# One directly loaded chunk in place of two, its transfers divided by partitions over two queues

## The chip, the cores and the metric

The kernel runs on one core of one Trainium2 chip. The metric is the device time of one execution in microseconds (us); lower is better. The four executions shown took between 714.0 and 714.33 us, with a median of 714.04 us.

The core has these engines: TensorE for matmuls (PE in the profile, its weight loads apart as PEld), VectorE (DVE), ScalarE (ACT), GpSimd (POOL) and SyncE (SP). DMA transfers are issued by an engine onto its queue and carried out by 16 DMA engines. In this kernel SyncE and ScalarE issue onto a hardware queue each (q1 and q10 in the profile), GpSimd onto a software queue (q0). The loads on GpSimd's queue can change the type on the way, here from fp32 to fp16.

## The reference

Two stages, one feeding the other. The first is a cross-covariance attention over channels, for each of 4 batches; the second an MLP with a squared ReLU over all 24320 tokens.

```python
# q, k, v: (4, 6080, 256) float32, tau = 1.0
qn = q / (np.linalg.norm(q, axis=1, keepdims=True) + 1e-06)
kn = k / (np.linalg.norm(k, axis=1, keepdims=True) + 1e-06)
s = kn.transpose(0, 2, 1) @ qn / tau            # 256 x 256 for each batch
a = softmax(s, axis=-1)
x = (v @ a).reshape(24320, 256)
h = x @ w_in                                    # 256 -> 2048
r = np.maximum(h, 0.0)
out = (moe_s * (r * r) + moe_b) @ w_out         # 2048 -> 256
```

## The kernel before, in words

For each batch the kernel needs the 256 x 256 product of k and q over 6080 rows (the Gram matrix) and the sums of squares of every column of q and k. From these it makes the attention matrix and folds it into w_in at once, so that the MLP's first matmul takes v directly: `wa` is that folded weight, and `mm1` (line 751) multiplies it with v transposed. The MLP runs in 48 groups of 512 tokens (the last of 256) and 16 steps to a group; the batches after the first have their Gram work laid between these steps by a table of step numbers (`at_step`). Batch 0 can't be hidden that way: nothing of the MLP can start before its Gram matrix is complete. It is worked through ahead of the loop, and this is the part that the change touches.

Batch 0's rows are cut into 13 chunks: 11 of 512 rows (128 partitions, 4 rows each), one of 256 and one of 192 (96 partitions). A chunk has two transfers, k and q. `Gram.load` (lines 120 to 134) issues them in one of two ways:

- Chunks below `NDIRECT` (line 97) are loaded directly: k by SyncE's queue and q by ScalarE's, as fp32, 512 KB each, into the staging tile `raw32` (line 491), which lies in a slot of the pool that later holds the MLP's activations. `Gram.cast` then makes fp16 of them: DVE casts k (line 139), ACT casts q (line 140).
- All others are loaded by GpSimd's queue (line 133), which casts on the way: 512 KB of fp32 are read and 256 KB of fp16 written.

GpSimd issues in program order: chunks 2 to 9, k and q of each in turn; then k of the last three chunks and q of the last three; then v's first group, five pieces of w_in, and v, w_out and two scalars. The chunks' fp16 tiles come from a pool of 8 buffers (`qk_pool`), which w_out's four pieces use afterwards.

For each chunk but the last three, the order of work on the engines (lines 551 to 559) is: eight matmuls of the Gram matrix (line 149, two for each of 4 rows); on some chunks one or two matmuls on constant data (`keep_busy`, line 544); squares of k on ACT (line 180); squares of q on DVE for even chunks (line 177) and on ACT for odd ones; two folding additions on DVE (line 194), and one that adds the result to chunk 0's (line 208). The last three chunks, the late ones, are ordered so that k's norms are complete first: squares, matmuls that sum them over the partitions (line 247), and four small ACT operations that make the inverse norm (line 272), while q of these chunks is still being loaded. Then come q's norms (line 251), the scaling, the exponentials and the first block of `wa` (lines 297 to 347), and with it the first MLP matmul.

Nearly every instruction is kept in program order on its engine (`po`). An engine that waits holds up all that stands behind it on that engine.

Of the kernel before, what the change touches and what calls it, by code (L numbers as in the profile page):

```python
# [17 lines left out]
def kernel(  # L18
# [12 lines left out]
    nc = tc.nc  # L31
    P = 128
# [23 lines left out]
    def po(ins):  # L56

        tc.keep_in_program_order(ins)
        return ins
# [34 lines left out]


    JC = 4
    NDIRECT = 2

    def make_chunks(rows_of):
        chunks, at = [], 0  # L100
# [11 lines left out]
    class Gram:  # L112
# [7 lines left out]
        def load(self, c, parts=(0, 1)):  # L120

            at, np_, jc = self.chunks[c]
            if 0 in parts:
                self.raw[c] = qk_pool.tile([P, 2, JC, C], FP16, tag="qk", name="qk")
            t = self.raw[c]
            direct = self.b == 0 and c < NDIRECT
            for i in parts:
                src = (k, q)[i]
                rows = src[self.b, at : at + np_ * jc, :].rearrange("(p j) c -> p j c", j=jc)
                if direct:  # L130
                    (nc.sync, nc.scalar)[i].dma_start(out=raw32[:, c, i], in_=rows)
                else:
                    po(nc.gpsimd.dma_start(out=t[:np_, i, :jc, :], in_=rows))
            self.tiles[c] = t[:, 1], t[:, 0]
# [355 lines left out]
    g0 = grams[0]  # L490
    raw32 = gpool.tile([P, NDIRECT, 2, JC, C], FP32, tag="g16", name="raw32")

# [4 lines left out]
    nc.vector.memset(eps, EPS)  # L497
    for c in range(NDIRECT):
        g0.load(c)
        g0.cast(c)  # L500
    for c in range(NDIRECT, len(g0.chunks) - NLATE):
        g0.load(c)
# [155 lines left out]
    for i, f in enumerate(folds):  # L658
        early.setdefault(FOLDS[i], []).append(f)
    at_step(14, lambda: po(nc.vector.tensor_scalar_mul(  # L660
        out=s_out, in0=s_bc, scalar1=1.0 / (LAM * LAM))))
# [357 lines left out]
```

## Time and profile before

| what | value |
|---|---|
| median of 4 executions | 714.04 us (714.0 to 714.33) |
| the profiled execution | 714.07 us, span 712.3 us from first to last instruction |
| TensorE's mean granted clock | 0.997 |
| PE busy | 693.0 us, 97% of the span |
| the two DVE casts of k, each | 0.69 us, starting at 5.98 and 9.59 us |
| the two ACT casts of q, each | 1.04 us, starting at 6.15 and 9.95 us |
| direct loads, issue to landing | 5.2 to 8.7 us |
| first and last issue of batch 0's loads on GpSimd | 1.42 and 26.43 us |
| first MLP matmul (L751) | 37.29 us |

Reading the profile: "L149" is line 149 of the kernel. A group's row gives the engine, the operation, the written tile, the read tile and the number of instructions. In square brackets or behind an arrow stands what ended the idle time before an instruction. A DMA share of 1 means that all 16 DMA engines had a packet in work throughout; it can pass 1, since packets of one engine overlap. GB/s counts the bytes written; a load that casts reads twice what it writes.

### The profile page before, as it was taken

To read this page: it belongs to the slowest core of one execution; us is meant where nothing else is said; L and a number is where in the kernel's file an instruction comes from. 1 tells how busy PE (TensorE), PEld (TensorE's weight loads), DVE (VectorE), ACT (ScalarE), POOL (GpSimd) and SP (SyncE) were. 2 spreads that over 40 slices of the span, in tenths; PEclk is the share of its full clock that TensorE was granted. 3 is DMA by queue.
4 is the path that set the end of the run, shared out by engine and by line. 5 is a ranking of instruction groups with operands and counts; after the bars stand their busy time and mean duration, and the time that the engine had idled before them with its cause. 6 is when DMAs were issued, how large, how long until landed. Compare 5 with 4: busy or idle time off the path is not lost.

```text
span 712.3 us, 17529 instructions
## 1 busy us (share of the span) xinstructions
PE 693.0 (97%) x7422; PEld 502.5 (71%) x7422; DVE 635.3 (89%) x905; ACT 548.5 (77%) x599; POOL 113.6 (16%) x192
## 2 busy tenths in 40 slices
PE   4699999999999999999999999999999999999998
PEld 2456777776677777777677777777768777777777
DVE  4889999999988989998999899998998888888886
ACT  5789877787787777778877777777876777777875
POOL 4533132202102222111010222111000000000000
PEclk9999999999999999999999999999999999999999
DMA  9999999556665977465761888637423333321202
GB/s 235 207 258 171 178 166 140 116 100 122 124 116 105 139 139 149 102 96 102 153 129 50 149 139 148 126 76 97 101 64 75 94 71 75 97 61 46 83 31 75
DMA packets 87838, 83.81 MB, mean 118 GB/s; under 512 B 56352, under 2 KB 62768, under 8 KB 87760
## 3 DMA queue, kind: packets, MB, share of 16 engines
q0 software_dynamic: 26992, 43.74, 38.1%
q1 hardware_dynamic: 60192, 37.71, 22.1%
q8 instruction: 58, 0.95, 0.6%
q10 hardware_dynamic: 576, 1.25, 0.5%
q14 instruction: 20, 0.16, 0.1%
HBM read 78.91 MB, written 24.90 MB: 146 GB/s over the span
## 4 chain that ended last, share of the span: by engine, by line
PE 95%; DMA 3%; ACT 1%; DVE 1%; issue 0%; DVEq 0%; ACTq 0%
PE h_ps L751 46%; PE o_ps L922 40%; PE s_ps L149 4%; DMA qk<-in_k_dram 1%; PE wa_ps L389 1%; DMA raw<-in_q_dram 1%; PE o_ps L826 1%; ACT sq L180 1%; PE o_ps L798 0%; PE wa_ps L331 0%; DVE f L194 0%; ACT r L272 0%; PE n_ps L247 0%; ACT qk L140 0%; DVE f L208 0%
## 5 line engine op out<-in xcount | busy, mean ns | idle before, releaser
L761 ACT ACTIVATE r<-h_ps 128x1024 f16<-128x1024 f32 (+1 forms) x384 | 388.5, 1013 | 144.2 <-PE h_ps L751 140.5
L751 PE MATMUL h_ps<-vT,wa 128*128 128x512 f16 (+7 forms) x1632 | 452.1, 364 | 0.5 <-ACT wa L324 0.5
L922 PEld LDWEIGHTS <-S 128*128 128x128 f16 x2944 | 198.1, 98 | 84.3
L922 PEld LDWEIGHTS <-g 128*128 128x128 f16 x2208 | 155.0, 98 | 74.1
L774 DVE TENSOR_TENSOR g<-r 128x2048 f16<-128x2048 f16 (+2 forms) x150 | 174.9, 1166 | 10.0 <-ACT r L761 9.5
L922 PE MATMUL o_ps<-T,S 128*128 128x128 f16 x2208 | 183.2, 219 | 0.0
L751 PEld LDWEIGHTS <-wa 128*128 128x128 f16 x1632 | 136.5, 98 | 19.0 <-ACT wa L324 1.0
L922 PE MATMUL o_ps<-w_out,g 128*128 128x128 f16 x1472 | 134.3, 219 | 0.0
L772 ACT ACTIVATE g<-r 128x1024 f16<-128x1024 f16 (+1 forms) x97 | 100.3, 1034 | 0.2
L779 DVE SCALAR_TENSOR_TENSOR o_sb<-o_ps,s_out,u 128x256 f32<-128x256 f32 x138 | 66.6, 482 | 36.0 <-PE o_ps L922 34.2
L149 PE MATMUL s_ps<-qk 128*128 128x256 f16 (+1 forms) x384 | 71.4, 287 | 14.5 <-ACT qk L140 9.2
L453 POOL DMA_DIRECT2D v<-in_v_dram x48 | 31.4, 663 | 238.7 <-DMA vT<-v 164.9
L210 POOL DMA_DIRECT2D f<-f x33 | 28.8, 874 | 248.1 <-DVE f L194 205.5
L779 DVE SCALAR_TENSOR_TENSOR u<-o_ps,s_out,rowconst 128x256 f32<-128x256 f32 x138 | 66.1, 479 | 0.0
L922 PE MATMUL o_ps<-w_out,S 128*128 128x128 f16 x736 | 63.5, 219 | 0.0
L922 PE MATMUL o_ps<-N,g 128*128 128x128 f16 x736 | 63.4, 219 | 0.0
L851 DVE TENSOR_TENSOR S<-S,g 128x2048 f16<-128x2048 f16 (+1 forms) x47 | 56.5, 1201 | 1.2
L180 ACT ACTIVATE sq<-qk 128x1024 f16<-128x1024 f16 (+2 forms) x53 | 54.5, 1041 | 3.9 <-DMA qk<-in_k_dram 2.2
L849 DVE TENSOR_TENSOR S<-g 128x2048 f16<-128x2048 f16 (+1 forms) x47 | 56.1, 1194 | 0.0
L855 DVE TENSOR_TENSOR S<-g,S 128x2048 f16<-128x2048 f16 x46 | 56.0, 1218 | 0.0
L853 DVE TENSOR_TENSOR S<-g 128x2048 f16<-128x2048 f16 x46 | 56.0, 1217 | 0.0
L149 PEld LDWEIGHTS <-qk 128*128 128x128 f16 (+1 forms) x384 | 32.7, 103 | 20.5 <-ACT qk L140 9.6
(103 smaller groups left out, 335.6 us busy)
## 6 DMA issues: line engine op xcount, KB each, us to landing
out_dram<-o_sb SPq DMA_DIRECT2D x43, 512.0 KB, 3.0
v<-in_v_dram POOLq DMA_DIRECT2D x47, 256.0 KB, 4.9
qk<-in_k_dram POOLq DMA_DIRECT2D x42, 256.0 KB, 6.6
qk<-in_q_dram POOLq DMA_DIRECT2D x42, 256.0 KB, 7.4
f<-f POOLq DMA_DIRECT2D x30, 128.0 KB, 2.9
vT<-v SPq DMA_TRANSPOSE x182, 3.1
w<-in_moe_w_out_dram POOLq DMA_DIRECT2D x4, 512.0 KB, 10.1
out_dram<-o_sb SPq DMA_DIRECT2D x8, 256.0 KB, 4.8
```

What stands on the lines that cost most here:

```text
L149: po(nc.tensor.matmul(self.s_ps[:, ch, :], qc[:np_, j, ts(ch, P)], kc[:np_, j, :], start=(c == 0 and j == 0 and ch == 0), stop=(c == len(s ...
L180: po(nc.scalar.activation(out=st["sq"][:np_, a, js, :], in_=(qc, kc)[a][:np_, js, :], func=AF.Square))
L751: po(nc.tensor.matmul(dst, wa[:, ci, ts(m, P)], src, start=(ci == 0), stop=(ci == CH - 1), skip_group_check=True))
L761: po(nc.scalar.activation(out=r16[:, :, i % 2, :n], in_=h_tiles.pop((g, i))[:, :, :n], func=AF.Relu))
L772: po(nc.scalar.activation(out=dst, in_=src, func=AF.Square))
L774: po(nc.vector.tensor_mul(dst, src, src))
L779: po(nc.vector.scalar_tensor_tensor(out=dst, in0=src, scalar=s_out, op0=ALU.mult, in1=add, op1=ALU.add))
L849: po(nc.vector.tensor_add(T[1], A21, A22))
L851: po(nc.vector.tensor_sub(T[2], T[1], A11))
L853: po(nc.vector.tensor_sub(T[3], A11, A21))
L855: po(nc.vector.tensor_sub(T[4], A12, T[2]))
L922: po(nc.tensor.matmul(st[name][:, j, :], a()[:, i, ts(j, P)], w[:, i, :], start=first, stop=last, skip_group_check=True))
```

## The change

`NDIRECT` goes from 2 to 1: only chunk 0 is loaded directly and cast by DVE and ACT, and chunk 1 goes by GpSimd's queue, ahead of chunk 2. `raw32` is half as large. Each of chunk 0's two transfers is divided by partitions: SyncE issues partitions 0 to 63 and ScalarE partitions 64 to 127, of k first and then of q. So SyncE and ScalarE still issue two transfers each, of 256 KB in place of 512 KB, and GpSimd issues two more than before. `ts(h, 64)` is the slice of 64 partitions from 64 h on; k is `i = 0`, q is `i = 1`.

```diff
     JC = 4
-    NDIRECT = 2
+    NDIRECT = 1
...
                 rows = src[self.b, at : at + np_ * jc, :].rearrange("(p j) c -> p j c", j=jc)
                 if direct:
-                    (nc.sync, nc.scalar)[i].dma_start(out=raw32[:, c, i], in_=rows)
+                    for h, queue in enumerate((nc.sync, nc.scalar)):
+                        ps = ts(h, P // 2)
+                        queue.dma_start(out=raw32[ps, c, i], in_=rows[ps])
                 else:
                     po(nc.gpsimd.dma_start(out=t[:np_, i, :jc, :], in_=rows))
```

## The prediction

> **What bounds the kernel now.** I read the page first, its busy shares and the shares of the chain that ended last, to see which stage the change touches; then the chain from its start; then the load stage in windows of 1 us, because a chain names one wait where several may stand behind each other. The page:
>
> ```profile
> PE 693.0 (97%) x7422; PEld 502.5 (71%) x7422; DVE 635.3 (89%) x905; ACT 548.5 (77%) x599; POOL 113.6 (16%) x192
> ...
> PE 95%; DMA 3%; ACT 1%; DVE 1%; issue 0%; DVEq 0%; ACTq 0%
> ```
>
> TensorE carries 95% of the chain, but not its beginning. The chain from the start, as start, length, what:
>
> ```profile
> 1.19 8.73 DMA raw<-in_q_dram
> ...
> 9.95 1.04 ACT qk L140
> ...
> 20.47 9.47 DMA qk<-in_k_dram
> 29.97 1.07 ACT sq L180
> ...
> 37.29 0.60 PE h_ps L751 x2
> ```
>
> Until the first MoE matmul at 37.29 us the chain hangs on batch 0's loads: the second direct load of q, then a GpSimd load of k issued at 20.47 and landed at 29.97. After 37.29 TensorE is busy without a break, so the change is worth the shift it gives to 37.29. Next, what the loads wait for (columns: window, length, busy time of PE, PEld, DVE, ACT, POOL, granted clock, DMA share, GB/s written):
>
> ```profile
> 2.00:3.00 1.00, 0.00 (x0) 0.00 (x0) 0.00 (x0) 0.02 (x1) 1.00 (x3) 1.00 0.72 111
> 3.00:4.00 1.00, 0.00 (x0) 0.00 (x0) 0.00 (x0) 0.00 (x0) 1.00 (x3) 1.00 0.95 356
> 4.00:5.00 1.00, 0.00 (x0) 0.00 (x0) 0.00 (x0) 0.00 (x0) 1.00 (x3) 1.00 1.04 426
> 7.00:8.00 1.00, 0.75 (x4) 0.57 (x5) 0.00 (x0) 0.19 (x1) 0.00 (x0) 1.00 1.07 352
> 20.00:21.00 1.00, 0.01 (x1) 0.00 (x0) 0.94 (x2) 0.69 (x2) 0.53 (x1) 1.00 1.11 207
> ```
>
> The DMA share is at 1 or above from 4 us on, and from 10 to 30 us the rate stays at 209 GB/s written. Those loads read fp32 and write fp16, so 209 written is 418 GB/s read; the direct loads write what they read, 426. Counted in fp32 bytes the 16 DMA engines do the same work either way, without a pause: the stage is bound by the DMA stream, and a wait for an issue is hidden behind what is in flight. GpSimd's issues show how much that is:
>
> ```profile
> 1.42 0.67 POOL L133 DMA_DIRECT2D qk<-in_k_dram  x1
> ...
> 5.20 0.60 POOL L133 DMA_DIRECT2D qk<-in_q_dram  x1
> 10.37 0.53 POOL L133 DMA_DIRECT2D qk<-in_k_dram  x1 [4.57 <-DMA qk<-in_k_dram]
> ...
> 20.47 0.53 POOL L133 DMA_DIRECT2D qk<-in_k_dram  x1 [0.97 <-ACT sq L180]
> ```
>
> Eight are issued by 5.80 us, the ninth waits for the first to land, and so on. One load is 512 KB of fp32, 1.25 us at 418, so eight are 10 us of work. Last, when the GpSimd queue (q0) begins to move data beside the two hardware queues (packets, MB, share of the 16 engines; window 5 to 6 us):
>
> ```profile
> q1 hardware_dynamic: 60, 0.20, 48.6%
> q10 hardware_dynamic: 57, 0.17, 42.6%
> q0 software_dynamic: 12, 0.02, 12.9%
> ```
>
> In windows of 0.2 us its first two packets fall in 5.6 to 5.8 and ten more in 5.8 to 6.0. The queue was issued to at 1.42: 4.2 us pass before a byte.
>
> **The change part by part.**
>
> Moved: chunk 1 (k and q, 1.05 MB of fp32) goes from the hardware queues to GpSimd's. DMA time 1.05 / 0.426 = 2.46 us before, 1.05 / 0.418 = 2.51 after: +0.05 us. The mixed windows (352 GB/s written at 7 to 8 us, of which 0.29 MB direct and 0.06 MB cast, so 0.41 read) lie between and change nothing.
>
> The gap: before, the hardware queues have moved 0.04, 0.11, 0.36 and 0.43 MB in the windows from 1 to 5 us, 0.94 of chunk 0's 1.05; the rest at 0.41 MB/us is through at 5.3. Before, chunk 1 follows on the same queues. After, only GpSimd's loads follow, at 5.7 to 5.8. The engines stand still for 0.4 to 0.5 us: +0.45. Below, 0: if the hardware traffic is what delays q0, it starts when they end. Above, 1.1, if q0's thin first packets (2 in one window of 0.2 us, 12 in the first 0.4, against 20 to 31 of all queues in a window) mean a ramp of 0.6 us more. I take 0.45, the row itself.
> The Trainium skill ("DMA: Bandwidth & Descriptors", section "Specifications") gives about 1 us to the first byte on the GpSimd path. By it q0 would start at 2.4, chunk 0 would leave no gap, and the sum would be 0.45 lower. The trace has 4.2 us and decides.
>
> The division: k and q of chunk 0 go as four transfers of 64 partitions, SP and ACT two issues each as before (0.38 to 0.45 us each), the same 4 KB rows and bytes on two queues. No transfer of before covers 64 partitions. At best they run at the 426 GB/s of the undivided pair: 0, and I see no reason for a gain, as those windows are full. At worst they fall to the lowest steady rate that the stage writes, 209: 1.05 / 0.209 = 5.0 us in place of 2.46, +2.55, which swallows the gap. I take +0.1, near the row with the same two queues and the same packets, and keep both ends.
> The Trainium skill ("SBUF — State Buffer", section "Can I just issue two DMAs to hit both halves?") speaks against the change: two concurrent transfers, one to each half of the partitions, gave only 6% more than one, and one transfer over all 128 is advised. With its 196 GB/s for 64 partitions that is 208 GB/s and a sum of about +2.6. No row here shows it.
>
> GpSimd: two more issues of 0.53 to 0.67 us, ahead of the rest. It has issued eight by 5.80 either way, chunks 1 to 4 in place of 2 to 5; chunk 5 then waits for chunk 1's k, due at 5.7 + 1.25 + 0.25 = 7.2. With some 10 us in flight this is nothing on the path; were the queue empty, each would cost its 0.53. Everything behind on that queue (v, w_in, w_out) keeps its place in the byte stream and moves with it.
>
> Casts: one DVE cast (0.69 us) and one ACT cast (1.04) go, and chunk 0's squares, which stood behind casts waiting for 9.59 and 9.95, start about 3 us sooner. DVE is behind by several us at first (chunk 2's q squared at 15.40) and caught up at 29.3, where it waits 0.51 us for ACT, and ACT for loads. Worth 0: k's chunk 10 still lands when the stream brings it. If the stream were not the limit, up to 2.5 us of gain (rival B).
>
> Matmuls: chunk 1's wait for the landing, not for the cast, at about 8.5 in place of 11.04. 0, as PE waits 1.2 to 1.5 us for each chunk's q from 18 to 26 us. The staging tile is half as large inside a slot of the same pool; 0.
>
> Sum: 0.05 + 0.45 + 0.1 = +0.6 us at every landing after chunk 0, and so at 37.29. The profiled execution took 714.07 us (span 712.3, 1.8 around it), 0.03 over the median of the four runs, 714.04. 714.07 + 0.6 = 714.7.
>
> **The rivals.**
>
> A, slower: the halves hold each other up. Place: chunk 0's load, 2.5 to 5.3 us; price up to +2.55, 716.6. It decides when the pair falls below 1.05 / (2.46 + 1.38) = 0.27 MB/us, where the sum passes 0.2% (1.43 us), about what a measurement of this kernel can tell from no change. For: nothing in the profile excludes it. Against: two queues at once reached 426.
>
> B, faster: the chain as printed is a chain of dependence. Chunk 1's q is usable at 5.7 + 2.5 + 0.25 = 8.45 in place of 9.95 + 1.04 = 11.0; ACT and DVE move up 2.5 us, the issue of 20.47 with them, and 29.97 becomes 27.5: 711.6. For: the row names an ACT square as releaser. Against: that GpSimd issue comes about 0.6 us after the load eight places before it lands, as its neighbours do, and a rate of 209 from 10 to 30 us leaves no gap to fill.
>
> C, the clock. These rows (same columns) show TensorE at half clock and back:
>
> ```profile
> 22.20:25.60 3.40, 1.54 (x11) 0.89 (x9) 3.16 (x8) 2.70 (x3) 1.45 (x4) 1.00 1.12 210
> 25.60:29.10 3.50, 2.90 (x12) 1.87 (x13) 3.26 (x7) 1.90 (x3) 1.30 (x4) 0.52 1.11 207
> 29.10:32.50 3.40, 2.31 (x19) 1.64 (x18) 2.59 (x7) 2.26 (x3) 2.75 (x4) 1.00 1.19 204
> ```
>
> After a stretch only 45% busy the clock halves; after one 83% busy it is back. Now it costs nothing, under the loads. Chunk 1's matmuls leave the block of 11.04 to 15.98, so the swings may move. If the half clock lay over 29.1 to 32.5, the norm matmuls on the chain (0.95 us) or all 2.31 busy us would double: with the 0.6, 715.6 to 717.0, middle 716.0. Against: from chunk 5 on the matmuls come when the loads land, as before, and the stretch before 29.1 holds four filling matmuls.
>
> D, no gap: q0 was late only because of the hardware traffic. 0.15 is left: 714.2.
>
> **How the numbers follow.** The forecast 0.42, A 0.25, D 0.17, B 0.08, C 0.08. The forecast's own range is 714.2 to 715.5 (gap 0 to 1.1 and division 0 to 0.3). Faster by over 0.2% (below 712.6) is B, 0.08. Slower by over 0.2% (above 715.47) is A and C, 0.33, and 0.05 from the forecast's upper end, 0.38. Within: 0.54. The range leaves B out and reaches from a little under D to A: 713.8 to 716.7.
>
> **What would show it.** Right: DMA packets thin out between 5.3 and 5.8 us; chunk 0's halves land by 6.2 and the first cast of q starts there; chunk 1's k lands near 7.2; the load of k's chunk 10 lands at about 30.6, and the first L751 matmul starts near 37.9; from there on both profiles run in parallel. A would show as less than 270 GB/s at 3 to 5 us and a cast of q after 7 us; B as a landing of chunk 10 before 29 with a rate above 418 read; C as a clock of 0.5 after 29.1; D as q0 packets before 5.5. I am wrong if the time after 37 us differs between the two by more than the shift, or if q0's start depends on how many loads GpSimd has been given.

## The result, and the profile after

The changed kernel takes 714.9 us (median of 41 executions, 714.58 to 716.55) against 714.19 us before (61 executions beside it, 713.76 to 715.38): a ratio of 1.0011, with a 95% interval of 1.0006 to 1.0015. It is slower by 0.7 us between the medians and 0.8 by the ratio, which is within the 0.2% that the prediction called no change, and 0.2 us from the forecast of 714.7. The profiled execution's span went from 712.3 to 713.1 us.

Nearly all of it arises before the first MLP matmul. The chain that ended last, of the changed kernel (start, length, what; L753 is the line that was L751):

```profile
2.10 7.28 DMA qk<-in_q_dram
...
9.66 9.74 DMA qk<-in_q_dram
...
21.21 9.46 DMA qk<-in_k_dram
...
30.69 1.07 ACT sq L182
...
38.06 0.60 PE h_ps L753 x2
```

The load of k's chunk 10 lands at 30.67 in place of 29.94 (the prediction's 29.97 is the start of the square that waits for it), and the first MLP matmul starts at 38.06 in place of 37.29: 0.77 us of the 0.8. Behind it the two profiles run in parallel: the last output piece that DVE makes starts at 710.23 against 709.45, 0.78 later. As the prediction had it, the DMA stream shifts everything. How the shift came about is another matter. The first casts and the issues on GpSimd's queue, from the timeline of the changed kernel (start, length, instruction, in brackets the wait before it):

```profile
0.74 0.57 SPq L133 DMA_DIRECT2D raw<-in_k_dram  x1
...
5.70 0.69 DVE L141 CAST qk<-raw 128x1024 f16<-128x1024 f32 x1 [3.99 <-DMA raw<-in_k_dram]
8.77 0.54 POOL L135 DMA_DIRECT2D qk<-in_k_dram  x1 [2.96 <-DMA qk<-in_k_dram]
8.93 1.04 ACT L142 CAST qk<-raw 128x1024 f16<-128x1024 f32 x1 [6.91 <-DMA raw<-in_q_dram]
```

The hardware queues have half as much to bring as before, and yet chunk 0's q is cast at 8.93 us; before it was 6.15. The transfers have become slow. The queues of the changed kernel from 4 to 5 us and from 5 to 6 us (packets, MB, share of the 16 DMA engines):

```profile
q1 hardware_dynamic: 24, 0.10, 44.6%
q0 software_dynamic: 34, 0.07, 36.7%
q10 hardware_dynamic: 31, 0.06, 30.4%
...
q1 hardware_dynamic: 38, 0.15, 55.8%
q0 software_dynamic: 42, 0.08, 44.2%
q10 hardware_dynamic: 1, 0.00, 1.8%
```

and the kernel before from 4 to 5 us:

```profile
q10 hardware_dynamic: 54, 0.22, 52.8%
q1 hardware_dynamic: 55, 0.21, 50.9%
```

The engines are busy in both, but on q1 one packet of 4 KB takes 0.446 x 16 / 24 = 0.30 us, where before it took 0.528 x 16 / 54 = 0.16 on q10. By the same division it is 0.27 on q10 from 3 to 4 us, before GpSimd's queue sends anything, and 0.23 on q1 from 5 to 6. And the queues take turns: from 3.6 to 4.0 us only q10 moves data, and from 5 to 6 q1 sends 38 packets and q10 one. Against that, GpSimd's queue (q0) now sends its first packet at 4.0 us and not at 5.7. There is no gap between the hardware queues' data and GpSimd's; there is a stretch, from 2 to 8 us, in which the engines are busy and slow. Counted in fp32 bytes (hardware bytes, and twice what q0 writes), some 1.05 + 2 x 0.36 = 1.77 MB have come by 8 us, against 1.87 + 2 x 0.15 = 2.17 before. The missing 0.4 MB are about 1 us at 418 GB/s, an estimate, of which 0.7 is seen when chunk 10 lands.

### The profile page after: what moved, and what is told of

It is laid out like the page before. It is cut to its first block, busy times and chain, and to the rows that moved or that the text cites. A ratio compares the mean times of both kernels' runs of the same rounds, so it can differ in the third digit from the quotient of the medians.

```text
span 713.1 us, 17531 instructions
## 1 busy us (share of the span) xinstructions
PE 692.0 (97%) x7422; PEld 502.1 (70%) x7422; DVE 634.8 (89%) x904; ACT 547.6 (77%) x598; POOL 114.7 (16%) x194
## 4 chain that ended last, share of the span: by engine, by line
PE 95%; DMA 4%; ACT 1%; issue 0%; POOL 0%; DVE 0%; POOLq 0%; ACTq 0%
PE h_ps L753 46%; PE o_ps L924 40%; PE s_ps L151 5%; DMA qk<-in_q_dram 2%; DMA qk<-in_k_dram 1%; PE wa_ps L391 1%; PE o_ps L828 1%; PE o_ps L800 0%; PE wa_ps L333 0%; ACT r L274 0%; PE n_ps L249 0%; ACT sq L182 0%; POOL qk L135 0%; ACT eT L305 0%; PE vT_ps L466 0%
## 5 line engine op out<-in xcount | busy, mean ns | idle before, releaser
L753 PE MATMUL h_ps<-vT,wa 128*128 128x512 f16 (+7 forms) x1632 | 452.1, 364 | 0.5 <-ACT wa L326 0.5
L753 PEld LDWEIGHTS <-wa 128*128 128x128 f16 x1632 | 136.6, 98 | 19.0 <-ACT wa L326 1.0
```

The lines of the kernel that those rows point to most:

```text
L753: po(nc.tensor.matmul(dst, wa[:, ci, ts(m, P)], src, start=(ci == 0), stop=(ci == CH - 1), skip_group_check=True))
```

## The experiments

The measure used below is the start of the first MLP matmul in a profile, since whole times differ by a few tenths of a us from execution to execution. They also hold what lies behind the last matmuls, the stores of the last outputs: from the start of the last group of matmuls to the end of the span it is 5.4 us in the kernels before and after, but 5.6 in the undivided run below, 5.7 in the one with whole transfers on SyncE's queue and 6.4 in the one without a direct load. So a time can move by more than its first matmul. Each edit is shown against the changed kernel. "Theory H" is that the halves are slow; "theory G" is the forecast's gap.

**Both kernels once more.** No edit.

> The kernel before once more, for the spread of the places that are read from a profile: first MLP matmul within 0.1 us of 37.29, casts of chunk 0 within 0.1 us of 5.98 and 6.15. If these wander by more than 0.3 us, differences between the other profiles of that size mean nothing.

> The changed kernel once more: first MLP matmul within 0.1 us of 38.06, casts of chunk 0 within 0.2 us of 5.70 and 8.93. A wander of more than 0.3 us would put the loss of 0.77 us in doubt.

Before: 37.20, casts of chunk 0 at 5.88 and 6.05, 714.0 us. After: 38.02, casts at 5.64 and 8.80, 714.84 us. The readings repeat within 0.13 us, and the shift is 0.82 in this pair and 0.77 in the first.

**The move without the division.**

```diff
-                    for h, queue in enumerate((nc.sync, nc.scalar)):
-                        ps = ts(h, P // 2)
-                        queue.dma_start(out=raw32[ps, c, i], in_=rows[ps])
+                    (nc.sync, nc.scalar)[i].dma_start(out=raw32[:, c, i], in_=rows)
```

> One chunk directly, undivided: k by SyncE's and q by ScalarE's queue, 128 partitions each. Only the move of chunk 1 is left of the change. Theory H (the halves): the cost of 0.77 us at the first MLP matmul comes from the division, whose four transfers take turns at 230 to 280 GB/s; without it the two queues run together at about 420 GB/s, both casts of chunk 0 start by 6.2 us, and the first MLP matmul stands at 37.3 to 37.5. Theory G (the forecast's gap): the GpSimd queue's first bytes come at 5.7 us, the engines stand still from 5.3 on, and the first MLP matmul stands at 37.8; the time is 0.45 to 0.5 us over that of the kernel before. If the move itself were the cost, 38.06 as in the changed kernel.

First MLP matmul at 37.12, chunk 10 landed at 29.77, casts at 5.86 and 6.01; 714.33 us against 714.02, ratio 1.0004 (0.9995 to 1.0013). The queues from 4 to 5 us and from 5 to 6 us:

```profile
q10 hardware_dynamic: 57, 0.23, 55.7%
q1 hardware_dynamic: 55, 0.19, 47.2%
q0 software_dynamic: 1, 0.00, 1.1%
...
q0 software_dynamic: 81, 0.17, 87.5%
q10 hardware_dynamic: 31, 0.07, 16.7%
q1 hardware_dynamic: 11, 0.01, 3.4%
```

The move of chunk 1 costs nothing; by the place of the first matmul it gains 0.1 to 0.2 us, which the times don't confirm (0.3 us slower, with an interval that holds no change). Theory G falls: the hardware queues run out over the window from 5 to 6 us, but q0 sends its first packet at 4.95 and takes 87.5% of that window. By the place of the first matmul the whole loss of 0.77 comes with the division, which costs 38.06 - 37.12 = 0.94 us. By the times it is less, 714.9 against 714.33 or 0.6 us, and the intervals of the two ratios overlap.

**The division without the move.**

```diff
-    NDIRECT = 1
+    NDIRECT = 2
```

> Two chunks directly as before, but each transfer divided into 64 and 64 partitions: only the division is left of the change. Theory H: twice as much goes by the slow halves, so the loss of the stream is about doubled, less what the GpSimd queue moves beside it: first MLP matmul at 38.3 to 39.0, 1.0 to 1.7 us over the kernel before, and chunk 1's q lands after 12 us. Theory G, or the move as the cost: within 0.2 us of 37.29, since there is no gap and nothing is moved.

First MLP matmul at 40.78, 3.5 us over the kernel before; 717.94 us against 714.02, ratio 1.0055 (1.0041 to 1.0069). The direction is theory H's, the size is twice what it expected. Chunk 1's q is cast at 14.21. The chain shows what the expectation left out:

```profile
2.91 11.22 DMA raw<-in_q_dram
14.21 1.04 ACT qk L142
...
18.14 0.70 DVE f L196
...
34.21 0.42 DVE f L196
34.64 0.35 DVE half L226
```

Chunk 1's lateness reaches the folds on DVE (chunk 1's own starts at 18.14 in place of 13.87), and from 18.14 to 35 us DVE waits for nothing. In the kernel before it had just caught up with the loads, at 29.3 us.

**The same with chunk 0's work ahead of chunk 1's casts** (against the kernel of the experiment just told).

```diff
-    for c in range(NDIRECT):
-        g0.load(c)
-        g0.cast(c)
+    g0.load(0)
+    g0.load(1)
+    g0.cast(0)
+    g0.start()
+    first_ops = g0.norm_ops(0)
+    for j in range(JC):
+        g0.mm(0, j)
+    for f in first_ops:
+        f()
+    g0.cast(1)
...
-    g0.start()
...
-    for c in range(NCH0 - NLATE):
+    for c in range(1, NCH0 - NLATE):
```

> Two chunks directly and divided, as in the run that stood at 40.78 us, but chunk 0's matmuls, squares and folds are put before chunk 1's casts in the engines' order. Theory V (in that run the late cast of chunk 1 held up chunk 0's folds on DVE, which then worked without a break from 16.24 to 35 us and became the bound): DVE's folds begin about 5 us sooner, near 11 us, DVE catches up with the loads before the late chunks, and what is left is the loss of the DMA stream alone, first MLP matmul at 38.3 to 39.3, no more than 2 us over the kernel before. Rival: the stream itself lost 3.5 us by the divided transfers; then it stays at 40.5 to 40.9.

First MLP matmul at 39.12, 716.55 us against 713.96, ratio 1.0035 (1.0022 to 1.0048). The order of the casts was worth 1.66 us of the 3.5, as theory V said. Its other half failed: DVE did not catch up. These lines of DVE's timeline show it waiting for chunk 1 a second time, and then working without a break until the late chunks:

```profile
12.79 0.69 DVE L141 CAST qk<-raw 128x1024 f16<-128x1024 f32 x1
16.48 0.69 DVE L196 TENSOR_TENSOR f<-sq 128x1024 f16<-128x1024 f16 x1 [3.00 <-ACT sq L182]
...
32.55 0.42 DVE L196 TENSOR_TENSOR f<-f 128x512 f16<-128x512 f16 x1
32.89 0.42 DVE L226 TENSOR_TENSOR half<-sq 128x512 f16<-128x512 f16 x1
```

What the stream alone lost with two divided chunks can't be read from the first matmul of either run, because DVE ended later than the stream in both, but the bytes give an estimate. By 20 us, in fp32 bytes, 2.10 + 2 x 2.54 = 7.18 MB have come in the kernel before and 2.10 + 2 x 2.23 = 6.56 in both of these: 0.62 MB, or 1.5 us at 418 GB/s, lie in theory H's range. By the same count the changed kernel lacks 0.37 MB, or 0.9 us.

**Even and odd partitions in place of lower and upper.**

```diff
-                        ps = ts(h, P // 2)
-                        queue.dma_start(out=raw32[ps, c, i], in_=rows[ps])
+                        queue.dma_start(out=raw32[h::2, c, i], in_=rows[h::2])
```

> As the changed kernel, but the two transfers of k and of q take the even and the odd partitions in place of the lower and the upper 64: the same 256 KB, 64 rows of 4 KB, queues and order. Theory H in its narrow form (it matters which 64 partitions a transfer covers): each transfer now reaches all over the partitions, the two queues run side by side at about 420 GB/s, q's cast starts by 6.2 us, first MLP matmul at 37.3 to 37.5. Rival S (size: transfers of 256 KB or of 64 rows on two queues take turns whatever they cover): as the changed kernel, about 250 GB/s, q's cast at 8.9, 38.0.

First MLP matmul at 37.84, casts at 4.71 and 7.71; 714.7 us against 714.02, ratio 1.0013 (1.0005 to 1.0022). Neither expectation holds. The queues from 3 to 4 us:

```profile
q10 hardware_dynamic: 69, 0.24, 65.0%
q1 hardware_dynamic: 35, 0.09, 25.4%
q0 software_dynamic: 9, 0.02, 11.4%
```

A packet on q10 takes 0.650 x 16 / 69 = 0.15 us, against 0.829 x 16 / 49 = 0.27 in the changed kernel's window from 3 to 4 us. Some of the 69 are short ones; a window in which all of q10's are of 4 KB is that from 5 to 6 us:

```profile
q0 software_dynamic: 43, 0.09, 46.9%
q1 hardware_dynamic: 36, 0.11, 31.2%
q10 hardware_dynamic: 26, 0.11, 28.1%
```

Here it is 0.281 x 16 / 26 = 0.17, close to the 0.16 of whole transfers: which 64 partitions a transfer covers bears on the time of a packet. The two queues also send side by side here, where the changed kernel's took turns (38 packets against one). What stays is a late start of q10: from 2 to 3 us it sends one packet against 51 on q1, where the undivided run has 9 against 25. Of the 0.94 us only about 0.2 come back.

**Divided by rows.** Each queue takes two of the four rows of all 128 partitions.

```diff
-                        ps = ts(h, P // 2)
-                        queue.dma_start(out=raw32[ps, c, i], in_=rows[ps])
+                        js = ts(h, JC // 2)
+                        queue.dma_start(out=raw32[:, c, i, js], in_=rows[:, js])
```

> As the changed kernel, but each transfer is divided by rows: two of the four rows of every partition on SyncE's queue and two on ScalarE's, 256 KB over 128 partitions each, rows of 2 KB in one piece. Theory H: all partitions are covered, so the queues run together; 2 KB pieces may cost a little; q's cast by 6.4 us, first MLP matmul at 37.3 to 37.7. Rival S (size of the transfer): q's cast at 8.9 us, 38.0.

First MLP matmul at 37.05, casts at 4.57 and 5.96; 714.51 us against 714.02, ratio 1.0005 (0.9996 to 1.0014). The number of transfers, their 256 KB, the queues and the order are those of the changed kernel, so it is not the size: it is that a transfer covers 64 partitions (and so has 64 rows of 4 KB where this one has 128 of 2 KB; no run here parts the two). The first issues of this kernel, and then those of the even and odd one:

```profile
0.74 0.38 SPq L133 DMA_DIRECT2D raw<-in_k_dram  x1
```

```profile
0.74 0.58 SPq L132 DMA_DIRECT2D raw<-in_k_dram  x1
```

A transfer of 64 partitions takes 0.57 to 0.63 us to issue in the kernels here (ScalarE's second one 0.85), one of 128 partitions 0.38 to 0.45, and the first packet comes at 2.1 to 2.3 us against 1.75 to 1.85. This kernel brings k earliest of those with two queues; neither its time nor that of the undivided one can be told from the kernel before.

**All on SyncE's queue, in halves.**

```diff
-                    for h, queue in enumerate((nc.sync, nc.scalar)):
+                    for h in range(2):
                         ps = ts(h, P // 2)
-                        queue.dma_start(out=raw32[ps, c, i], in_=rows[ps])
+                        nc.sync.dma_start(out=raw32[ps, c, i], in_=rows[ps])
```

> As the changed kernel, but all four half transfers go by SyncE's queue, in the order k lower, k upper, q lower, q upper. Theory H: in the changed kernel the halves take turns anyway, each at 230 to 280 GB/s, so the second queue bought nothing: casts near 5.7 and 8.9 us, first MLP matmul at 37.9 to 38.4. Rival Q (it is two queues with one half each that hold each other up): on one queue the halves follow each other at full rate, q's cast by 7 us, first MLP matmul at 37.2 to 37.5.

First MLP matmul at 38.41, casts at 7.06 and 10.36; 715.39 us against 714.06, ratio 1.0016 (1.0006 to 1.0025). Rival Q falls: the halves are slow on one queue too. They are a little slower than on two (0.35 us at the first matmul), and theory H's casts were expected more than 1 us too early: the second queue did buy something. The profiled execution, 716.62 us, was the slowest of the ten; in it TensorE also waits 1.25 us for a load of q that lands at 116.5 us, which is no part of what is compared here.

**All on SyncE's queue, whole.**

```diff
-                    for h, queue in enumerate((nc.sync, nc.scalar)):
-                        ps = ts(h, P // 2)
-                        queue.dma_start(out=raw32[ps, c, i], in_=rows[ps])
+                    nc.sync.dma_start(out=raw32[:, c, i], in_=rows)
```

> One chunk directly, undivided, k and then q both by SyncE's queue. Theory H: whole transfers of 128 partitions run at about 400 GB/s one after the other, so k lands well before q; casts near 4.6 and 6.2 us, first MLP matmul at 37.0 to 37.5. Rival Q would have the same here. If one queue alone can't fill the 16 engines, the rate before 5 us stays under 300 GB/s, q's cast comes after 7 us, and the first MLP matmul at 37.6 to 38.1.

First MLP matmul at 37.44, casts at 4.22 and 5.63; 714.76 us against 714.06, ratio 1.001 (1.0 to 1.0019). The queues from 3 to 4 us:

```profile
q1 hardware_dynamic: 109, 0.38, 95.5%
```

One queue with whole transfers fills the 16 engines alone. Between one queue in halves and one queue whole lie 0.97 us, the same as between two queues in halves and two whole (0.94). The time is 0.7 us over the kernel before although the first matmul is only 0.15 later; in the profiled execution (714.54 us) the rest lies behind the last matmul. And by 8 us this kernel has brought 1.05 + 2 x 0.64 = 2.33 MB in fp32 bytes, more than the 2.17 of the kernel before, and still k's chunk 10 lands 0.15 us later (30.09): the count of bytes tells the place of a landing only to some tenths of a us.

**No direct load.** All of batch 0 by GpSimd's queue.

```diff
-    NDIRECT = 1
+    NDIRECT = 0
...
-    raw32 = gpool.tile([P, NDIRECT, 2, JC, C], FP32, tag="g16", name="raw32")
```

> No chunk directly: all of batch 0 by the GpSimd queue, no hardware transfer at the start and no casts. It shows when that queue starts by itself, issued to at 1.42 us. Theory W (its start waits on the hardware traffic: 5.65 us beside full hardware queues, 4.1 beside the halves): its first bytes come at 2.5 to 3.5 us, chunk 0's k lands by 4.8, and the whole stream is late only by its later start, first MLP matmul at 37.3 to 38.3. Theory O (its start has its own delay, whatever the others do): first bytes at 4.1 to 5.7 us, nothing moves before, and the first MLP matmul comes at 39 to 40.5, 2 to 3 us over the kernel before.

First MLP matmul at 38.76; 716.4 us against 714.08, ratio 1.0032 (1.002 to 1.0043). GpSimd's queue, issued to at 1.43 us, sends its first packet at 2.8 us. Theory W holds for the start; the first matmul is 0.5 us later than its range. Of the 2.3 us in time, about 1 arises behind the last matmul in the profiled execution, among the stores of the last outputs; its cause is open. The first packet of q0 over the runs, in us: 2.8 with no direct load and 2.83 with halves on one queue; 3.7, 4.0 and 4.1 with halves on two queues (even and odd, the changed kernel, two chunks; 3.85 with two chunks in the other order of work); 4.6, 4.7 and 4.95 with one chunk in whole transfers or by rows; 5.6 to 5.7 with two whole chunks. It comes later beside fast transfers than beside slow ones, and latest with two whole chunks; beside halves on one queue it is not late at all. What holds it back in the chip the profile doesn't show.

## Why the prediction was right, and where its working was wrong

- What bounds the stage: right. DMA share and rate from 10 us on are as before (209 GB/s from 10 to 20 us against 210), and everything behind the loads moved by the shift of the stream. Casts, matmuls, GpSimd's issues and the chunk's move were put at nothing or 0.05 us; the undivided run shows -0.17 for all of them and the gap together.
- The gap, "the engines stand still for 0.4 to 0.5 us: +0.45": wrong. The step that failed took q0's start at 5.7 us, read beside two full hardware queues, for a delay of its own. The prediction's lower bound for this term, 0, had the reason right ("if the hardware traffic is what delays q0"), and that was rival D, at 0.17; its sign, packets of q0 before 5.5 us, came in both the changed kernel (4.0) and the undivided one (4.95). In place of the gap the runs show none: in the undivided kernel q0 takes over at 87.5% of the engines while the hardware queues run out. The Trainium skill ("DMA: Bandwidth & Descriptors", section "Specifications") gives about 1 us to the first byte on this path; alone on the engines it took 1.4 (1.43 to 2.8), beside two full queues 4.2. The row that I let decide held only beside those full queues.
- The division, taken at +0.1 "near the row with the same two queues and the same packets": mis-sized. It measured 0.94. The value lay inside the bounds of 0 and 2.55, but I chose the wrong end: the packets were the same in size and not in time (0.23 to 0.30 us against 0.16).
- Rival A: the loss arose in its place, chunk 0's load. Its signs came: 283 GB/s written from 3 to 4 us and 229 from 4 to 5, 256 over both, GpSimd's own 0.07 MB included, and a cast of q at 8.93 and so after 7. That two halves hold each other up is only part of it: they were slow on one queue too. Its price did not come; q0 began at 4.0 and had brought 0.72 MB of fp32 beside the halves by 8 us. The Trainium skill ("SBUF — State Buffer", section "Can I just issue two DMAs to hit both halves?") says that two such transfers serialize, and the 38 packets against one from 5 to 6 us agree; the sum of +2.6, an estimate that I made from its figure, left out the traffic beside them.
- Rival B: nothing of it is seen. ACT and DVE did begin ahead of the loads, and DVE waited for work from 24 us on (0.43 us busy in the window from 24 to 25, against 0.97 before); the stream didn't move. Two of the experiments show the other side of this: with chunk 1's first fold 2.6 us later than before (16.48 against 13.87) or 4.3 us later (18.14), DVE was the bound.
- Rival C: the half clock moved from 25.6 to 29.1 us to a window from 27 to 30.5. It stayed under the loads and cost nothing that the chain shows. The "middle 716.0" of its range was miscounted: between 715.6 and 717.0 lies 716.3.
- The signs that the prediction named for itself: the late ones came, chunk 10 at 30.67 for 30.6 and the first MLP matmul at 38.06 for 37.9. The early ones failed: from 5 to 6 us the queues' shares sum to 1.02 and nothing thins out, q was cast at 8.93 in place of 6.2, and chunk 1's k landed at about 8.8 in place of 7.2. The lower end of the forecast's own range, with gap and division at 0, should have been 714.1 in place of 714.2.

So 714.7 came out near 714.9 by luck, from two wrong terms: 0.5 for the gap and the move where the undivided run shows -0.17, and 0.1 for the division where it shows 0.94. The errors nearly cancel, and so the time lies even in the forecast's own range, 714.2 to 715.5. What was right for its reason is that the DMA stream sets the first MLP matmul.

## What to carry to other kernels

Divide a transfer so that each part still covers all partitions, by rows within the partition; a division by halves of the partitions took the time of a packet from 0.16 to as much as 0.30 us here and made the parts take turns. Where the DMA engines are the bound, work taken off DVE and ACT was worth no more than 0.2 us and a second queue 0.3; count the bytes that have come by a given time, and take the count as an estimate. A queue's start that was read beside other traffic says nothing about its start without it.

## What was unexpected

A transfer of 64 partitions is slow in a second way, beside where it lies: with even and odd partitions a packet was nearly as fast as in whole transfers (0.17 us against 0.16) and the loss still 0.72 us against the undivided run. Longer issues (0.58 against 0.38 us), a later first packet on both queues and a start of q10 only when most of q1's first transfer is through are seen; which of them makes the loss is open. GpSimd's queue began anywhere from 1.4 to 4.2 us after its first issue, late beside whole transfers on the hardware queues, early without them.
